# Odd periods of an attention loop: the second piece of the two-piece score tile goes to TensorE third instead of fourth, the first dense half product fourth

## The chip, the cores and the metric

One Trainium2 chip, one core of it. The metric is device microseconds of the whole program. Before the change three runs took 1686.16, 1686.31 and 1686.96 us; their median is 1686.31 us.

## The reference

Everything is float32, with one batch of S = 2048 tokens, width D = 512, 32 heads of 16 channels, and a gated hidden layer of F = 1792.

```python
def _A_ref(x, wqkv, wo):                                   # softmax attention, 32 heads of 16
    qkv = ((x @ wqkv).reshape(B, S, 3, H, Dh)).transpose(2, 0, 3, 1, 4)
    q, k, v = qkv[0], qkv[1], qkv[2]
    scores = einsum("bhqd,bhkd->bhqk", q, k) * Dh ** -0.5
    p = softmax(scores, axis=-1)
    o = einsum("bhqk,bhkd->bhqd", p, v)
    return o.transpose(0, 2, 1, 3).reshape(B, S, D) @ wo

def _B_ref(x, w_gate, w_up, w_down):                       # gated hidden layer
    return (sigmoid(x @ w_gate) * (x @ w_up)) @ w_down

g = sigmoid((x * gate_w).sum(-1, keepdims=True))           # one gate per token
out = g * _A_ref(x, wqkv, wo) + (1 - g) * _B_ref(x, w_gate, w_up, w_down)
```

## The kernel before, in words

**Stages.** A start (to about 85 us) makes the queries, keys and values that the first head pair needs. Then comes a long loop of 256 periods, `for k in range(NPER)`, and after it a last stage with the down projection and the output projection. The change is inside the first 248 periods (`NPER - TAIL`), which use the two strings of `STEADY`; the last eight use `LAST`, which is not touched.

**What a period does.** The heads are worked on in 16 pairs, each pair in 16 periods. A period handles, for the pair, 512 queries against 512 keys, and on TensorE it holds four kinds of work:

- *score tiles* (`t0`, `t1`; L641 in `st_part`): key rows times query columns, one 128x512 tile into a PSUM bank. ScalarE (ACT) takes each tile out with an exponential (L643, into `p`). Each period runs two calls of `st_part`, of four tiles each. The first tile of each period is written in two pieces of 192 and 320 columns (`CUT`), each with its own bank and its own exponential, so a period has nine score matmuls and nine exponentials.
- *maximum tiles* (`m0`, `m1`; L299 in `sm_step`): scores once more with the queries as rows, 128x512, some periods ahead of their use; VectorE (DVE) takes the row maxima (L301, into `stat`). Eight per period.
- *dense half products* (`d0`, `d1`; L153 and L173, into the one bank `dn`): projections of queries and keys, then the gate and up projections, then the start of the down projection, each contracting over 64 of the 128 rows. Twelve per period. ACT takes a finished `dn` out (L574).
- *value products* (L781 in `values`): 32 small matmuls after the written order of the period, with exponentials as their moving operand: those of the first score call of this period and of the second call of the period before. ACT copies the result out (L786), into `sum` for the first of four periods of a part and into `part` for the other three, which POOL then adds.

**Two halves of the array.** Tokens with a 0 use the lower 64 rows of TensorE's array, tokens with a 1 the upper 64, and the two halves work at the same time. In even periods the score tiles are on the lower half with six of the maximum tiles, and the dense products on the upper half; in odd periods it is the other way round.

**What sets the order.** All compute engines run what the program text emits, in that order (a manual schedule). `emit` reads a string of `STEADY` word by word, `STEADY[0]` for even k and `STEADY[1]` for odd k, and each word emits one matmul with what follows it (for `t` the matmul and its exponential on ACT, for `m` the matmul and its maximum on DVE, for `d` the matmul alone). The word `work` lets POOL take one of the jobs that wait in `later`. After the string come the run's change-over (`next(fill)`, with the copy out of `dn` on ACT), some POOL jobs, and `values(k)`.

**Banks.** Score tiles, maximum tiles and the value product take seven PSUM banks in turn (`place = turns(seven)`), each in the order in which it is emitted; a dense product takes no bank of these. A period takes 9 + 8 + 1 = 18 turns, so a matmul's bank is the one that was taken seven turns earlier, and it has to wait until ACT or DVE has read that one.

Of the kernel before, what the change touches and what calls it, by code (L numbers as in the profile page):

```python
# [51 lines left out]
def gated_mix(ctx, tc, x, xc, xmix, wqk, wv, wo, w_gu, w_down, gate_w, out):  # L52
# [768 lines left out]
    def emit(order, **parts):  # L821

        for word in order.split():
# [7 lines left out]
            else:  # L831
# [1 line left out]
                    place()  # L833

    STEADY = ("t0 m1 t0 d1 t0 d1 m0 d1 t0 m0 d1 d1 t0 d1 work t0 m0 d1 t0 d1 m0 d1 t0 d1 m0 d1 t0 d1 m1 m0",
              "t1 m0 d0 t1 t1 d0 m1 d0 t1 d0 m1 t1 d0 d0 work d0 t1 m1 t1 d0 d0 d0 m1 t1 d0 m1 t1 d0 m1 m0")
    LAST = ["t0 d1 t0 d1 t0 d1 t0 d1 d1 work t1 t1 t1 t1", "t0 d1 t0 d1 t0 d1 t0 d1 work t1 t1 t1 t1"] * 2 + [
        "t0 t0 t0 t0 work t1 d0 t1 d0 t1 d0 t1 d0 d0", "t0 t0 t0 t0 work t1 d0 t1 d0 t1 d0 t1 d0"] * 2

# [214 lines left out]
```

## Time and profile before

| what | before |
|---|---|
| median of 3 runs | 1686.31 us (1686.16 to 1686.96) |
| the profiled execution, its own time | 1686.26 us |
| its span in the trace | 1684.5 us |
| PE busy (matmuls) | 1678.5 us, 16842 instructions |
| DVE busy | 1429.2 us |
| ACT busy | 1346.9 us |
| POOL busy | 1054.2 us |

How to read it: the span is cut by engine into instructions. PE is TensorE's matmuls, PEld its weight loads, SP the queue that issues DMAs. A row of a timeline has the start in us from the span's start, the duration, the engine, the line of the kernel, the operation, the output and input tiles with their buffer numbers left out, and the count of instructions that were merged into the row; in square brackets stands the idle time of the engine ahead of it and what released it. Matmuls overlap in the pipeline and the end of each is modelled, so a PE that is busy all the time may still wait. A period is seen best on PE: each of the first 248 has exactly one 64x192 score matmul, its first instruction, so the distance between two of these is the length of a period.

### The profile page before, as it was taken

How to read it: one execution, taken by the hardware profiler on the slowest of the kernel's cores; microseconds unless marked ns; L12 is line 12 of the kernel's file. 1: busy time of each engine (PE TensorE's matmuls, PEld its weight loads, DVE VectorE, ACT ScalarE, POOL GpSimd, SP SyncE). 2: the span in 40 equal slices, each digit the busy share in tenths (PEclk: the TensorE clock that was granted, in tenths of full speed). 3: DMA queues.
4: the chain of work that ended last, by engine and by line, in shares of the span. 5: the costliest groups of instructions: out<-in, count | busy, mean ns of one | idle time of the engine just before them, and what ended most of it. 6: DMA issues, size and time to landing. Idle time of an engine off the chain costs nothing.

```text
span 1684.5 us, 44610 instructions
## 1 busy us (share of the span) xinstructions
PE 1678.5 (100%) x16842; PEld 1165.1 (69%) x16842; DVE 1429.2 (85%) x2456; ACT 1346.9 (80%) x2928; POOL 1054.2 (63%) x1238
## 2 busy tenths in 40 slices
PE   9999999999999999999999999999999999999999
PEld 7866666666666666666666666666666666678887
DVE  6889898898989989899898998989989899668553
ACT  4188888888888888888888999999999988974321
POOL 1146665368878788776675897777776767742110
PEclk9999999999999999999999999999999999999999
DMA  9624667464444444442347353424242325269850
GB/s 257 132 80 157 190 201 195 130 158 139 121 145 133 127 139 127 127 117 71 96 147 204 128 141 102 123 87 97 97 102 92 106 83 182 68 220 305 294 178 25
DMA packets 131559, 236.74 MB, mean 141 GB/s; under 512 B 19408, under 2 KB 39888, under 8 KB 128336
## 3 DMA queue, kind: packets, MB, share of 16 engines
q1 hardware_dynamic: 131056, 233.37, 46.5%
q8 instruction: 133, 2.18, 0.6%
q14 instruction: 82, 0.67, 0.2%
q10 hardware_dynamic: 288, 0.52, 0.1%
HBM read 155.71 MB, written 77.59 MB: 139 GB/s over the span
## 4 chain that ended last, share of the span: by engine, by line
PE 99%; DVE 0%; ACT 0%; issue 0%; POOL 0%; ACTq 0%; DVEq 0%
PE dn L173 27%; PE sm L781 17%; PE st L781 12%; PE dn L153 8%; PE sm L299 7%; PE sm L990 6%; PE sm L641 6%; PE st L299 5%; PE st L641 4%; PE st L140 4%; PE dn L990 2%; PE st L153 1%; PE st L990 1%; PE st L88 0%; DVE stat L301 0%; ACT p L643 0%
## 5 line engine op out<-in xcount | busy, mean ns | idle before, releaser
L301 DVE TENSOR_REDUCE stat<-sm 128x1 f32<-128x512 f32 x1199 | 763.8, 682 | 85.6 <-PE st L641 56.1
L643 ACT ACTIVATE p<-sm 128x512 f32<-128x512 f32 (+1 forms) x1314 | 669.6, 588 | 6.8 <-PE sm L641 5.3
L301 DVE TENSOR_REDUCE stat<-st 128x1 f32<-128x512 f32 x849 | 549.8, 682 | 57.8 <-PE sm L641 57.4
L643 ACT ACTIVATE p<-st 128x512 f32<-128x512 f32 (+2 forms) x982 | 515.6, 588 | 1.8 <-PE st L641 0.5
L299 PE MATMUL sm<-ks,qs 48*128 48x512 f32 x1199 | 486.1, 429 | 0.1
L173 PE MATMUL dn<-xm,mh 64*128 64x512 f32 x1568 | 486.1, 390 | 0.0
L641 PE MATMUL sm<-qs,ks 64*128 64x512 f32 (+1 forms) x1314 | 471.5, 382 | 0.0
L299 PE MATMUL st<-ks,qs 48*128 48x512 f32 x849 | 365.7, 431 | 0.0
L641 PE MATMUL st<-qs,ks 64*128 64x512 f32 (+2 forms) x982 | 363.0, 382 | 0.6 <-DVE v L622 0.6
L173 PE MATMUL dn<-xm,ml 64*128 64x512 f32 x784 | 305.4, 389 | 0.0
L173 PEld LDWEIGHTS dn<-xm,mh 64*128 64x128 f32 x1568 | 289.5, 185 | 14.5
L641 PEld LDWEIGHTS sm<-qs,ks 64*128 64x128 f32 x1314 | 233.1, 186 | 75.5 <-DVE stat L301 58.4
L781 PE MATMUL sm<-p,v 128*17 128x256 f32 x4672 | 280.6, 380 | 0.1
L299 PEld LDWEIGHTS sm<-ks,qs 48*128 48x128 f32 x1199 | 211.0, 184 | 45.5 <-ACT p L643 38.9
L641 PEld LDWEIGHTS st<-qs,ks 64*128 64x128 f32 x982 | 177.0, 186 | 57.5 <-DVE stat L301 44.9
L781 PEld LDWEIGHTS sm<-p,v 128*17 128x17 f32 x4672 | 122.9, 97 | 130.2 <-ACT p L643 44.6
L781 PE MATMUL st<-p,v 128*17 128x256 f32 x3520 | 211.4, 380 | 0.2 <-ACT p L643 0.2
L799 POOL TENSOR_TENSOR sum<-sum,part 128x256 f32<-128x256 f32 x192 | 141.5, 737 | 78.8 <-ACT part L786 62.7
L424 POOL TENSOR_TENSOR m<-m,m 128x512 f32<-128x512 f32 x140 | 178.0, 1289 | 5.4 <-ACT m L574 3.3
L299 PEld LDWEIGHTS st<-ks,qs 48*128 48x128 f32 x849 | 156.5, 184 | 32.3 <-ACT p L643 29.2
L781 PEld LDWEIGHTS st<-p,v 128*17 128x17 f32 x3520 | 92.7, 97 | 98.3 <-ACT p L643 33.5
L173 PEld LDWEIGHTS dn<-xm,ml 64*128 64x128 f32 x784 | 144.2, 184 | 10.0
(314 smaller groups left out, 2342.3 us busy)
## 6 DMA issues: line engine op xcount, KB each, us to landing
r<-in_w_gu_dram SPq DMA_DIRECT2D x112, 256.0 KB
gul<-gu_d SPq DMA_DIRECT2D x56, 512.0 KB
gu_d<-m SPq DMA_DIRECT2D x84, 256.0 KB
xm_d<-xm SPq DMA_DIRECT2D x32, 512.0 KB
xm<-xm_d SPq DMA_DIRECT2D x32, 512.0 KB
xm<-in_xmix_dram SPq DMA_DIRECT2D x24, 512.0 KB
qs<-q_d SPq DMA_DIRECT2D x90, 128.0 KB
ks<-k_d SPq DMA_DIRECT2D x90, 128.0 KB
```

The source lines that it names most:

```text
L140: pe.matmul(o, a, b, start=(i == 0), stop=(i == len(ops) - 1))
L153: mm = pe.matmul(self.o, a[rows], b[rows], start=(self.n == 0), stop=(self.n == 2 * len(self.ops) - 1))
L173: pe.matmul(self.o, a, b, start=(self.n == 0), stop=(self.n == len(self.ops) - 1))
L299: pe.matmul(t, qs[r:r + KM, qt * P:(qt + 1) * P], ks[r:r + KM, g * 512:(g + 1) * 512], start=True, stop=True)
L301: dve.tensor_reduce(stat[part][:, qt % 4, g:g + 1], t, axis=AX.X, op=ALU.max)
L424: pool.tensor_tensor(o, x, y, op)
L641: pe.matmul(o, ks[r:r + KR, (kt + a) * P:(kt + a + 1) * P], qs[r:r + KR, c * 512 + lo:c * 512 + hi], start=True, stop=True)
L643: act.activation(pt[:, a, lo:hi], o, AF.Exp, scale=DH ** -0.5)
L781: pe.matmul(o[r:r + VW, :], v[:, 4 * k % 16 + a, h * VW:(h + 1) * VW], pts[b][:, a, 256 * i:256 * i + 256], start=(a == 0), stop=(a == 3))
L799: pool.tensor_tensor(s, s, e, ALU.add)
L990: pe.matmul(down[t], a, b, start=(f == 0 and m == 0), stop=(f == NF - 2 and m == 5))
```

## The change

In the string for odd periods two neighbouring words change places: `t1 m0 d0 t1 t1 d0 ...` becomes `t1 m0 t1 d0 t1 d0 ...`. The third matmul of an odd period is then the 320-column second piece of the score tile, and the fourth the first dense half product. The string for even periods, which begins `t0 m1 t0 d1 t0 d1`, is as it was.

```diff
     STEADY = ("t0 m1 t0 d1 t0 d1 m0 d1 t0 m0 d1 d1 t0 d1 work t0 m0 d1 t0 d1 m0 d1 t0 d1 m0 d1 t0 d1 m1 m0",
-              "t1 m0 d0 t1 t1 d0 m1 d0 t1 d0 m1 t1 d0 d0 work d0 t1 m1 t1 d0 d0 d0 m1 t1 d0 m1 t1 d0 m1 m0")
+              "t1 m0 t1 d0 t1 d0 m1 d0 t1 d0 m1 t1 d0 d0 work d0 t1 m1 t1 d0 d0 d0 m1 t1 d0 m1 t1 d0 m1 m0")
```

The order of the instructions on TensorE differs in 124 places, one in each odd period; the orders on ACT, DVE, POOL and SP are the same as before. The score pieces and maximum tiles keep their order among themselves, so every one of them keeps its bank.

The first such place, at the opening of period 1 on TensorE (`dn` is the bank of the dense products, `q1h` a weight of the query projection, `st` and `sm` the seven banks in turn):

```order
 L641 MATMUL st1_66<-qs0_101,ks0_102 128x192
 L299 MATMUL sm3_72<-ks0_102,qs0_101 128x512
+L641 MATMUL st0_65<-qs0_101,ks0_102 128x320
 L153 MATMUL dn_68<-xt0_130,q1h_366 128x512
-L641 MATMUL st0_65<-qs0_101,ks0_102 128x320
 L641 MATMUL sm0_69<-qs0_101,ks0_102 128x512
```

The 320-column piece has moved ahead of one dense product.

In the middle of the program, at the opening of period 129 on TensorE (the dense products are now those of the up projection, L173), before:

```order
L641 MATMUL sm3_72<-qs0_101,ks0_102 128x192
L299 MATMUL st0_65<-ks0_102,qs0_101 128x512
L173 MATMUL dn_68<-xm0_2_4461,mh2_0_5_1_11185 128x512
L641 MATMUL sm0_69<-qs0_101,ks0_102 128x320
L641 MATMUL sm1_70<-qs0_101,ks0_102 128x512
L173 MATMUL dn_68<-xm0_2_4461,mh2_0_5_1_11185 128x512
L299 MATMUL st2_67<-ks0_102,qs0_101 128x512
```

and with the change:

```order
L641 MATMUL sm3_72<-qs0_101,ks0_102 128x192
L299 MATMUL st0_65<-ks0_102,qs0_101 128x512
L641 MATMUL sm0_69<-qs0_101,ks0_102 128x320
L173 MATMUL dn_68<-xm0_2_4461,mh2_0_5_1_11185 128x512
L641 MATMUL sm1_70<-qs0_101,ks0_102 128x512
L173 MATMUL dn_68<-xm0_2_4461,mh2_0_5_1_11185 128x512
L299 MATMUL st2_67<-ks0_102,qs0_101 128x512
```

The same two instructions have changed places, with the same banks.

The opening of period 130, an even one, on TensorE, the same before and after:

```order
L641 MATMUL st2_67<-qs0_101,ks0_102 128x192
L299 MATMUL sm2_71<-ks0_102,qs0_101 128x512
L641 MATMUL st1_66<-qs0_101,ks0_102 128x320
L173 MATMUL dn_68<-xm0_2_4461,mh2_0_5_1_11185 128x512
L641 MATMUL sm3_72<-qs0_101,ks0_102 128x512
L173 MATMUL dn_68<-xm0_2_4461,mh2_0_5_1_11185 128x512
L299 MATMUL st0_65<-ks0_102,qs0_101 128x512
```

Nothing moved here; it stands for comparison, since an odd period now opens with the same kinds of instructions in the same order.

## The prediction

> **What bounds the kernel now.** I read the page first, then the list of waits, and then the timeline of two neighbouring periods engine by engine.
>
> ```profile
> span 1684.5 us, 44610 instructions
> PE 1678.5 (100%) x16842; PEld 1165.1 (69%) x16842; DVE 1429.2 (85%) x2456; ACT 1346.9 (80%) x2928; POOL 1054.2 (63%) x1238
> PEld sm L781 <- ACT p L643: 44.6, 146, 0.5
> PEld st L781 <- ACT p L643: 33.5, 109, 0.7
> ```
>
> The page makes PE busy all the time, but these are modelled ends. The waits say more: the value products (L781) waited for an exponential 146 + 109 = 255 times, which is once in each period but one. So every period ends with PE behind ACT, and the question is what ACT does in a period. First PE's timeline: an odd period (129, from 802.01) and the even one after it (from 807.60), to the start of the next.
>
> ```profile
> 802.01 0.35 PE L641 MATMUL sm<-qs,ks 64*128 64x192 f32 x1
> 802.01 0.50 PE L299 MATMUL st<-ks,qs 48*128 48x512 f32 x1
> 802.20 0.33 PE L641 MATMUL sm<-qs,ks 64*128 64x320 f32 x1
> 802.35 0.39 PE L173 MATMUL dn<-xm,mh 64*128 64x512 f32 x1
> ...
> 804.71 0.39 PE L299 MATMUL st<-ks,qs 48*128 48x512 f32 x1
> ...
> 804.88 0.39 PE L173 MATMUL dn<-xm,ml 64*128 64x512 f32 x1
> 804.94 0.39 PE L641 MATMUL sm<-qs,ks 64*128 64x512 f32 x1
> 805.26 0.50 PE L299 MATMUL st<-ks,qs 48*128 48x512 f32 x1
> 805.26 0.50 PE L299 MATMUL sm<-ks,qs 48*128 48x512 f32 x1
> 805.75 1.92 PE L781 MATMUL sm<-p,v 128*17 128x256 f32 x32
> 807.60 0.35 PE L641 MATMUL st<-qs,ks 64*128 64x192 f32 x1
> ...
> 807.94 0.40 PE L173 MATMUL dn<-xm,mh 64*128 64x512 f32 x1
> ...
> 811.24 1.92 PE L781 MATMUL sm<-p,v 128*17 128x256 f32 x32
> 813.09 0.35 PE L641 MATMUL st<-qs,ks 64*128 64x192 f32 x1
> ```
>
> The odd period lasts 807.60 - 802.01 = 5.59 us, the even one 813.09 - 807.60 = 5.49. From the value products to the next period both take 1.85 us (805.75 to 807.60, 811.24 to 813.09); the difference of 0.10 lies before them: 3.74 us in the odd period, 3.64 in the even one. Both hold nine score matmuls, eight maximum tiles and twelve dense products. It is not these two periods alone; the openings of periods 2 and 246 give the mean of the 122 pairs between them:
>
> ```profile
> 97.83 0.35 PE L641 MATMUL sm<-qs,ks 64*128 64x192 f32 x1
> 1450.62 0.35 PE L641 MATMUL st<-qs,ks 64*128 64x192 f32 x1
> ```
>
> (1450.62 - 97.83) / 122 = 11.09 us a pair. With 5.49 for the even period an odd one is 5.60 in the mean.
>
> Now ACT, the same two periods, in narrow windows so that rows aren't merged: the copy of the last value product, the exponentials of 192 and 320 columns, and the sixth and seventh exponential.
>
> ```profile
> 802.14 0.38 ACT L786 ACTIVATE sum<-st 128x256 f32<-128x256 f32 x1 [0.57 <-PE st L781]
> 802.46 0.33 ACT L643 ACTIVATE p<-sm 128x192 f32<-128x192 f32 x1
> 802.81 0.44 ACT L643 ACTIVATE p<-sm 128x320 f32<-128x320 f32 x1
> 804.58 0.63 ACT L643 ACTIVATE p<-st 128x512 f32<-128x512 f32 x1
> 805.05 0.65 ACT L643 ACTIVATE p<-sm 128x512 f32<-128x512 f32 x1
> ...
> 807.80 0.38 ACT L786 ACTIVATE part<-sm 128x256 f32<-128x256 f32 x1 [0.63 <-PE sm L781]
> 808.08 0.33 ACT L643 ACTIVATE p<-st 128x192 f32<-128x192 f32 x1
> 808.29 0.45 ACT L643 ACTIVATE p<-st 128x320 f32<-128x320 f32 x1
> 810.04 0.66 ACT L643 ACTIVATE p<-sm 128x512 f32<-128x512 f32 x1
> ```
>
> The value product's bank was taken seven turns earlier by the seventh score piece, so it starts when the seventh exponential is through: 805.05 + 0.65 = 805.70, and PE goes at 805.75. In between ACT runs without a break, a 512-column exponential every 0.47 us (804.58 to 805.05). A period is thus one chain: value product, its copy, seven exponentials, next value product. Whatever holds an early exponential is paid in full at the end.
>
> The two chains differ at one place. In the odd period ACT starts the 320-column exponential 0.35 us after the 192-column one (802.46, 802.81), and after that one's end (802.79). In the even period it starts 0.21 after it (808.08, 808.29), overlapping its last 0.12, as all later steps overlap (each 0.63 to 0.66 long, 0.47 apart). So in the odd period ACT is held by the 320-column matmul, and in the even one it isn't.
>
> **The change, part by part.** It removes and adds nothing; per odd period the 320-column piece goes ahead of one dense product. Three effects.
>
> *The 320-column exponential is released earlier.* In the odd period this matmul is emitted behind the dense product; that one ends at 802.35 + 0.39 = 802.74, and the exponential starts 0.07 later. In the even period the dense product is behind it and the exponential starts 808.29 - 807.94 = 0.35 after the dense product's start, before that has ended. The recorded start of the 320-column matmul itself (802.20) is ahead of the dense product (802.35), against the emitted order; I believe ACT's start, since ACT is what the chain waits for, and take it that the count ACT waits on passes the 320-column piece after the dense one. The Trainium skill, TensorE: Matmul & The Clock Gate, section "The mechanism", says that matmuls start and end strictly in program order; the ends seem to agree (released 0.07 us after the dense product's end), the recorded starts don't. By that rule the sum would be the same.
>
> The even period is then the price list for the changed odd one: 5.60 - 5.49 = 0.11 us saved.
>
> *Some odd periods can do better.* In period 129 the copy goes to `sum` and ACT takes it 0.13 us after the period's start (802.01, 802.14); a copy to `part` in period 130 comes at 0.20 (807.60, 807.80). In the odd period this head start is lost, since ACT then waits for the 320 columns anyway. A few even periods have the early copy; this one opens at 430.84:
>
> ```profile
> 430.84 0.35 PE L641 MATMUL sm<-qs,ks 64*128 64x192 f32 x1
> 430.98 0.38 ACT L786 ACTIVATE part<-st 128x256 f32<-128x256 f32 x1 [0.57 <-PE st L781]
> 431.29 0.33 ACT L643 ACTIVATE p<-sm 128x192 f32<-128x192 f32 x1
> 431.52 0.43 ACT L643 ACTIVATE p<-sm 128x320 f32<-128x320 f32 x1
> 436.30 0.35 PE L641 MATMUL sm<-qs,ks 64*128 64x192 f32 x1
> L786 ACT ACTIVATE sum<-sm 128x256 f32<-128x256 f32 x35 | 13.4, 384 | 20.6 <-PE sm L781 20.6
> L786 ACT ACTIVATE sum<-st 128x256 f32<-128x256 f32 x27 | 10.4, 384 | 15.3 <-PE st L781 15.3
> ```
>
> It copies at 0.14, starts the 320 columns at 0.68 (0.69 in the even period above, 0.80 in the odd one) and lasts 436.30 - 430.84 = 5.46 us. There are 35 + 27 = 62 copies to `sum`; `values` makes one after every fourth period, from 0 on, so it falls into the opening of an odd one. Hence 62 of the 124 odd periods come to 5.46, a saving of 0.14, and the other 62 to 5.49.
>
> *The dense product goes one place back.* It stays behind the same maximum tile on its half of the array and in the even period starts at 807.94 - 807.60 = 0.34, as in the odd one (802.35 - 802.01). The 320 columns' own bank has long been read. I cost it at nothing, covered by the maximum tile that runs ahead of it on the same half for 0.50 us; without that cover it would be the 0.2 us of the slower rival. Nothing is issued on SP or POOL by the words that change places.
>
> One period saves nothing: in the one that opens at 247.49 (its copy is at 247.62) the first exponential itself is late.
>
> ```profile
> 247.62 0.38 ACT L786 ACTIVATE sum<-sm 128x256 f32<-128x256 f32 x1 [1.06 <-PE sm L781]
> 248.22 0.33 ACT L643 ACTIVATE p<-st 128x192 f32<-128x192 f32 x1 [0.22 <-PE sm L641]
> ```
>
> The sum: 62 x 0.14 = 8.7, plus 62 x 0.11 = 6.8, less 0.1 for that period: 15.4 us. The profiled execution took 1686.26 us around a span of 1684.5, the median is 1686.31; they agree to 0.05, so the saving counts against either: 1686.3 - 15.4 = **1670.9 us**.
>
> Bounds for a period's saving. Above: 0.14, the shift of the exponential itself (0.35 less 0.21) and the shortest even period; 124 x 0.14 = 17.4 us, 1668.9. Below: ACT's visible gap in the odd period is only 802.81 - 802.79 = 0.02, if the overlap of the two exponentials can't be had there; 124 x 0.02 = 2.5 us, 1683.8. I take the even period's value, since it is measured on the same instructions with only the array halves exchanged.
>
> What is late next? DVE idles at the opening of both periods, so it has room for 0.14:
>
> ```profile
> 802.54 0.69 DVE L301 TENSOR_REDUCE stat<-st 128x1 f32<-128x512 f32 x1 [0.61 <-PE sm L641]
> 808.14 0.69 DVE L301 TENSOR_REDUCE stat<-sm 128x1 f32<-128x512 f32 x1 [0.45 <-PE st L641]
> ```
>
> POOL is busy for 63% of the span.
>
> **The rivals.**
>
> *PE's own pace takes over.* In the odd period the last two maximum tiles start at 805.26, 0.32 after the last score tile; at PE's step of 0.23 (804.71 to 804.94) they could at best go at 805.17. If that 0.09 is all, the gain is 124 x 0.09 = 11.2 us: 1675.1. Against it: the 5.46 us period has the same number of matmuls on each half.
>
> *No effect.* If the recorded starts are the truth, the array already runs the 320 columns (802.20) ahead of the dense product (802.35), and the late exponential has another cause that belongs to the odd order or the upper half. Then the time stays at 1686.3. Against it: the exponential's start just behind the dense product's end.
>
> *Slower: the piece blocks its own half's weights.* Emitted directly behind the 192 columns on the same half, it may have to wait until these are through (0.35) and its weights are in (0.19 to the next start, 802.01 to 802.20), and the dense product behind it would start at 0.54 instead of 0.34. Its half then still has that product, eleven more and a maximum tile to run; the last of these, due 0.23 after the last dense product (804.88), goes 0.20 later, at 805.31 instead of 805.26: 0.05 x 124 = 6.2 us, 1692.5. It decides as soon as the delay is over 0.15. Against it: the even period opens in this order and its dense product starts at 0.34. The Trainium skill, same page and section, has it that a weight load overlaps a running matmul only if the two are on different row groups, which would make this rival real; the even period disagrees, with the 0.34.
>
> **How the numbers follow.** Forecast as summed (1668.9 to 1673): 0.74. PE's pace or another part of the gain (1673 to 1682): 0.12. No effect: 0.09. Slower: 0.05. A measurement of this kernel can tell about 0.2%, 3.4 us, from no change. The first two cases are faster by more than that: 0.86; same 0.09; slower 0.05. The range takes the forecast's own bounds and the first rival's 1675.1 with some room: 1668.5 to 1677.
>
> **What would show it.** In the changed profile odd periods should open as even ones do: the 320-column exponential 0.21 to 0.23 us after the 192-column one, the value products 3.61 to 3.64 us after the period's start, and periods of 5.46 (after `sum`) and 5.49. The recorded starts on PE should hardly move. The pair falls from 11.09 to 10.96 in the mean. I am wrong if the exponential still starts 0.35 behind the first; or if it starts early and the value products still wait until 3.74, for another reason; or if the dense product starts at over 0.4.

## The result, and the profile after

The changed kernel took **1671.09 us** (median of 4 runs, 1670.84 to 1671.81) against 1686.24 us for the kernel before (4 runs, 1685.29 to 1686.96): a ratio of 0.9911, 95% interval 0.9894 to 0.9928. The profiled execution has a span of 1669.2 us, 15.3 less than the 1684.5 before.

The page and the waits of the changed kernel, in the lines that answer to those shown of before:

```profile
span 1669.2 us, 44610 instructions
PE 1663.4 (100%) x16842; PEld 1174.6 (70%) x16842; DVE 1427.2 (85%) x2456; ACT 1334.1 (80%) x2928; POOL 1052.3 (63%) x1238
PEld sm L781 <- ACT p L643: 44.6, 146, 0.5
PEld st L781 <- ACT p L643: 33.5, 109, 0.6
```

The counts of instructions and the 255 waits of the value products for an exponential are the same; what shrank is the time from one such wait to the next. PE's timeline, periods 129 and 130 again, and the openings of periods 131, 2 and 246:

```profile
794.03 0.35 PE L641 MATMUL sm<-qs,ks 64*128 64x192 f32 x1
794.04 0.50 PE L299 MATMUL st<-ks,qs 48*128 48x512 f32 x1
794.23 0.33 PE L641 MATMUL sm<-qs,ks 64*128 64x320 f32 x1
794.38 0.39 PE L173 MATMUL dn<-xm,mh 64*128 64x512 f32 x1
...
797.16 0.50 PE L299 MATMUL sm<-ks,qs 48*128 48x512 f32 x1
797.20 0.45 PE L299 MATMUL st<-ks,qs 48*128 48x512 f32 x1
797.64 0.41 PE L781 MATMUL sm<-p,v 128*17 128x256 f32 x4
...
799.49 0.35 PE L641 MATMUL st<-qs,ks 64*128 64x192 f32 x1
...
804.98 0.35 PE L641 MATMUL st<-qs,ks 64*128 64x192 f32 x1
...
97.48 0.35 PE L641 MATMUL sm<-qs,ks 64*128 64x192 f32 x1
1435.44 0.35 PE L641 MATMUL st<-qs,ks 64*128 64x192 f32 x1
```

The odd period 129 now lasts 799.49 - 794.03 = 5.46 us (5.59 before), the even one 804.98 - 799.49 = 5.49, as before. The pair is (1435.44 - 97.48) / 122 = 10.97 us in the mean (11.09 before). The value products start 797.64 - 794.03 = 3.61 us into the odd period (3.74 before). The recorded starts at the opening have not moved: 320 columns 0.20 after the 192, the dense product at 0.35.

ACT in the same odd period: copy, both pieces, seventh exponential; then the copy and the pieces of period 131, an odd one that opens at 804.98 with a copy to `part`:

```profile
794.17 0.39 ACT L786 ACTIVATE sum<-st 128x256 f32<-128x256 f32 x1 [0.57 <-PE st L781]
794.48 0.33 ACT L643 ACTIVATE p<-sm 128x192 f32<-128x192 f32 x1
794.71 0.43 ACT L643 ACTIVATE p<-sm 128x320 f32<-128x320 f32 x1
...
796.93 0.66 ACT L643 ACTIVATE p<-sm 128x512 f32<-128x512 f32 x1
...
805.18 0.38 ACT L786 ACTIVATE part<-sm 128x256 f32<-128x256 f32 x1 [0.63 <-PE sm L781]
805.46 0.33 ACT L643 ACTIVATE p<-st 128x192 f32<-128x192 f32 x1
805.67 0.45 ACT L643 ACTIVATE p<-sm 128x320 f32<-128x320 f32 x1
```

The 320-column exponential starts 0.68 us into period 129 (0.80 before), 0.23 after the 192-column one (0.35 before), and now overlaps its end (794.48 + 0.33 = 794.81). In period 131 it starts at 0.69, 0.21 after. The seventh ends at 796.93 + 0.66 = 797.59, and the value products go 0.05 later, as before.

DVE, the first maximum of periods 129 and 130:

```profile
794.57 0.69 DVE L301 TENSOR_REDUCE stat<-st 128x1 f32<-128x512 f32 x1 [0.62 <-PE sm L641]
800.03 0.69 DVE L301 TENSOR_REDUCE stat<-sm 128x1 f32<-128x512 f32 x1 [0.31 <-PE st L641]
```

Its idle time ahead of the even period's first maximum fell from 0.45 to 0.31 us and is not used up.

### The profile page after: what moved, and what is told of

Read it like the earlier page. It is cut to its first block, busy times and chain, and to the rows that moved or that the text cites. A ratio compares the mean times of both kernels' runs of the same rounds, so it can differ in the third digit from the quotient of the medians.

```text
span 1669.2 us, 44610 instructions
## 1 busy us (share of the span) xinstructions
PE 1663.4 (100%) x16842; PEld 1174.6 (70%) x16842; DVE 1427.2 (85%) x2456; ACT 1334.1 (80%) x2928; POOL 1052.3 (63%) x1238
## 4 chain that ended last, share of the span: by engine, by line
PE 99%; DVE 0%; ACT 0%; issue 0%; POOL 0%; ACTq 0%; DVEq 0%
PE dn L173 27%; PE sm L781 17%; PE st L781 13%; PE dn L153 7%; PE sm L299 6%; PE sm L641 6%; PE sm L990 6%; PE st L299 4%; PE st L641 4%; PE st L140 4%; PE dn L990 2%; PE st L153 2%; PE st L990 1%; PE st L88 0%; ACT p L643 0%; DVE stat L301 0%
## 5 line engine op out<-in xcount | busy, mean ns | idle before, releaser
L173 PE MATMUL dn<-xm,mh 64*128 64x512 f32 x1568 | 485.7, 389 | 0.0
L173 PE MATMUL dn<-xm,ml 64*128 64x512 f32 x784 | 304.7, 389 | 0.0
L173 PEld LDWEIGHTS dn<-xm,mh 64*128 64x128 f32 x1568 | 290.0, 185 | 15.9
L173 PEld LDWEIGHTS dn<-xm,ml 64*128 64x128 f32 x784 | 144.4, 184 | 10.3
```

Of the source, the lines that this page charges most:

```text
L173: pe.matmul(self.o, a, b, start=(self.n == 0), stop=(self.n == len(self.ops) - 1))
```

## The experiments

Six kernels ran. The first four were timed beside the kernel before at 1686.10 us (13 runs), the last two beside it at 1686.01 us (15 runs).

### The other half of the array: the old order in even periods

```diff
-    STEADY = ("t0 m1 t0 d1 t0 d1 m0 ...
+    STEADY = ("t0 m1 d1 t0 t0 d1 m0 ...
```

> The changed kernel, with the even periods opened as the odd ones were before (t0 m1 d1 t0 t0 d1): one dense product ahead of the 320-column piece, on the other halves of the array. Theory (one dense product ahead holds the 320-column exponential, whichever half): even periods go from 5.49 to 5.60 us, 124 x 0.11 = 13.6 us, 1684.7 us in all; the 320-column exponential in even periods starts at 0.80 instead of 0.69. Rival (it was something of the odd periods or the upper half): no change, 1671.1 us.

Measured: 1684.49 us (10 runs, 1683.79 to 1684.82), ratio to the kernel before 0.9990 [0.9981, 0.9999]; 13.4 us over the changed kernel where 13.6 were expected. PE at the opening of the even period 130 and of the next, and ACT's 320-column exponential in it:

```profile
806.72 0.35 PE L641 MATMUL st<-qs,ks 64*128 64x192 f32 x1
...
812.31 0.35 PE L641 MATMUL st<-qs,ks 64*128 64x192 f32 x1
...
807.52 0.44 ACT L643 ACTIVATE p<-st 128x320 f32<-128x320 f32 x1
```

The even period lasts 5.59 us and the exponential starts at 0.80. What cost time was the order, not something of odd periods or of the upper half; the even period was a fair price list. That this kernel is still 1.6 us under the kernel before also fits: the early copies to `sum` all open odd periods, which can now use them, and 62 periods of 5.46 us in place of 5.49 make about 1.4 us.

### A larger dose: two dense products ahead

```diff
-              "t1 m0 t1 d0 t1 d0 m1 d0 ...
+              "t1 m0 d0 d0 t1 t1 m1 d0 ...
```

> The changed kernel, with two dense products ahead of the 320-column piece in odd periods (t1 m0 d0 d0 t1 t1). Theory: the exponential is released by the end of the last dense product ahead, one step of 0.23 us later than with one: it starts at 0.58 + 0.39 + 0.07 = 1.04 us, odd periods take 5.60 + 0.23 = 5.83 us, 1686.2 + 124 x 0.23 = 1714.7 us. If the piece itself only had to start after the dense products: its end at 0.58 + 0.33 = 0.91, the exponential at 0.98, 124 x 0.06 less: 1707 us. Rival (order plays no part, the halves run apart): near 1686 us or below.

Measured: 1715.18 us (2 runs, 1714.84 to 1715.53), ratio 1.0173 [1.0153, 1.0193]. The opening of period 129 on PE, and ACT:

```profile
817.37 0.35 PE L641 MATMUL sm<-qs,ks 64*128 64x192 f32 x1
...
817.57 0.33 PE L641 MATMUL sm<-qs,ks 64*128 64x320 f32 x1
817.71 0.40 PE L173 MATMUL dn<-xm,mh 64*128 64x512 f32 x1
...
817.95 0.39 PE L173 MATMUL dn<-xm,mh 64*128 64x512 f32 x1
...
818.42 0.44 ACT L643 ACTIVATE p<-sm 128x320 f32<-128x320 f32 x1 [0.26 <-PE st L299]
```

The trace still puts the 320-column matmul at 817.57 to 817.90, but its exponential starts at 818.42, 1.05 us into the period, 0.08 after the second dense product's end (817.95 + 0.39 = 818.34). By these times ACT would have idled 0.26 us for nothing (the releaser named in the bracket, a maximum tile, is inferred from recorded ends). 1.04 was expected for a release by the end of what stands ahead, 0.98 for a release after its start.

### A short matmul ahead

An extra word `e0` between `m0` and the 320-column piece runs this method of `Side`, the class of the gate and up projections:

```diff
+        def probe(self):
+            if self.n == 0:
+                a, b = self.ops[0]
+                pe.matmul(self.o[:, :128], a, b[:, :128], start=True, stop=True)
...
-              "t1 m0 t1 d0 t1 d0 m1 ...
+              "t1 m0 e0 t1 d0 t1 d0 m1 ...
```

> The changed kernel, with an extra matmul of 128 columns of the first dense product's operands ahead of the 320-column piece, in the 98 odd periods of the gate and up projections; the product itself then overwrites it, so nothing is left out. Theory (the exponential is released by the end of what stands ahead): the short matmul starts at 0.34 and ends near 0.57, before ACT is free; the exponential starts at 0.67 to 0.69 as now, 1671 to 1673 us. Rival (the piece can't start before what stands ahead of it has started, at 0.34, so its size doesn't matter): the exponential starts near 0.74 to 0.80, 98 x 0.06 to 0.12 = 6 to 12 us, 1677 to 1683 us.

Measured: 1671.01 us (4 runs, 1670.48 to 1671.51), ratio 0.9910 [0.9893, 0.9926]. Period 129 (L179 is the added matmul; lines after it are shifted by some):

```profile
794.30 0.35 PE L646 MATMUL sm<-qs,ks 64*128 64x192 f32 x1
...
794.64 0.22 PE L179 MATMUL dn<-xm,mh 64*128 64x128 f32 x1
...
794.71 0.44 PE L173 MATMUL dn<-xm,mh 64*128 64x512 f32 x1
...
794.98 0.43 ACT L648 ACTIVATE p<-sm 128x320 f32<-128x320 f32 x1
```

The short matmul takes the place that the dense product had, starts at the same 0.34 and ends at 794.86, 0.56 us into the period. The exponential starts at 0.68. So it isn't the position behind a matmul of the other half that costs, nor that one's start, but its end: with 512 columns that came at 0.73, too late for ACT; with 128 columns it comes in time.

### One place further: the piece second

```diff
-              "t1 m0 t1 d0 t1 d0 m1 ...
+              "t1 t1 m0 d0 t1 d0 m1 ...
```

> The changed kernel, with the 320-column piece ahead of the first maximum tile too in odd periods (t1 t1 m0 d0). Theory: ACT is busy with the copy and the 192-column exponential until 0.67 us, so nothing more is to be had on its chain. If the halves of the array start apart from each other: the maximum tile starts at 0.00 as now, 1671.1 us. If starts are strictly in the emitted order: the maximum tile starts at 0.19, its half is 0.19 late to the end and the value products at least 0.10 us later: 1671.1 + 12.4 = 1683.5 us.

Measured: 1671.21 us (4 runs, 1670.78 to 1671.54), ratio 0.9912 [0.9897, 0.9927], no different from the change. PE and DVE in period 129, and ACT's 320-column exponential:

```profile
793.82 0.35 PE L641 MATMUL sm<-qs,ks 64*128 64x192 f32 x1
793.83 0.50 PE L299 MATMUL sm<-ks,qs 48*128 48x512 f32 x1
794.01 0.33 PE L641 MATMUL st<-qs,ks 64*128 64x320 f32 x1
...
794.42 0.69 DVE L301 TENSOR_REDUCE stat<-sm 128x1 f32<-128x512 f32 x1 [0.67 <-PE st L641]
...
794.50 0.43 ACT L643 ACTIVATE p<-st 128x320 f32<-128x320 f32 x1
```

The exponential stays at 0.68: ACT has nothing more to gain there. The maximum tile is recorded at the period's start, ahead of the piece that is emitted before it; it isn't 0.19 late, and the 12.4 us of that case are not there. But its consumer is released later: DVE starts at 0.60 instead of 0.54, 0.08 after the end of the 320-column piece (794.01 + 0.33 = 794.34). That is the same rule with the parts exchanged, on DVE, where the slack pays; the counts of TensorE's semaphore, given with the release below, bear it out.

### What is next on ACT's chain: the copy's second wait

The prediction found that a copy to `part` starts 0.06 us later than one to `sum`. Most copies to `part` wait for PE and also for POOL, which long since has read the buffer. The wait for POOL is put on an exponential at the end of a period, where ACT has a queue of work:

```diff
+    adds = []
...
-                act.activation(pt[:, a, lo:hi], o, AF.Exp, scale=DH ** -0.5)
+                e = act.activation(pt[:, a, lo:hi], o, AF.Exp, scale=DH ** -0.5)
+                if a == 3 and not first and len(adds) > 1:
+                    tc.add_manual_dep(e.ins, adds[-2].ins.name, SYNC, reason="part is free")
...
-            pool.tensor_tensor(s, s, e, ALU.add)
+            adds.append(pool.tensor_tensor(s, s, e, ALU.add))
```

> The changed kernel; the wait for POOL that 173 copies of the value product carry as a second wait (so that part is free again) is put on the last exponential of the period before the copy. Theory (ACT's chain still sets the period, and the second wait costs the copy 0.06 us, of which 5.49 - 5.46 = 0.024 us reaches the period): 173 x 0.024 = 4.2 us, 1666.9 us; late copies start 0.14 us after the period's start instead of 0.20, and nearly all periods take 5.46 us. Rival (PE's own pace now sets the period, and 5.46 is only had where the banks fall well): 1671.1 us.

Measured: **1667.10 us** (4 runs, 1666.68 to 1667.38), ratio to the kernel before 0.9887 [0.9874, 0.9901]; 4.0 us under the changed kernel where 4.2 were expected. Period 130, its copy, and the opening of the next:

```profile
797.42 0.35 PE L642 MATMUL st<-qs,ks 64*128 64x192 f32 x1
797.55 0.38 ACT L789 ACTIVATE part<-sm 128x256 f32<-128x256 f32 x1 [0.57 <-PE sm L784]
802.88 0.35 PE L642 MATMUL st<-qs,ks 64*128 64x192 f32 x1
```

The copy starts at 0.13 (0.20 before), idle 0.57 instead of 0.63 behind the value product, and the period lasts 5.46 us. Over periods 1 to 246, the 171 copies with the second wait start at 0.20 in the changed kernel (one of them at 0.47), while the 75 without it, 13 of them to `part`, start at 0.14; here all 246 start at 0.14. So the wait made the copy late, not the tile that it writes. ACT's chain still set the length of the periods that had the late copy. Only part of the 0.06 us arrives: the 192-column exponential starts 0.48 us into a period with the late copy and 0.45 into one with the early copy, and the period differs by about 0.02; what takes up the rest isn't shown. This version is faster than both kernels.

The same edit on the kernel before:

> The kernel before, with the same moved wait as the run before. Theory (in odd periods the 320-column exponential waits for PE at 0.80 us, so an earlier copy is lost there): only the 117 late even periods gain, 117 x 0.024 = 2.8 us, 1683.4 us; odd periods stay at 5.60 us. Rival (the head start counts in all periods): 173 x 0.024 = 4.2 us, 1682.0 us, with late odd periods at 5.57.

Measured: 1682.87 us (11 runs, 1682.11 to 1683.45), ratio 0.9982 [0.9973, 0.9991]. The gain, 3.1 us under this series' 1686.01, lies between the two that were expected, 2.8 and 4.2, and the time alone doesn't settle it. The trace does: periods 129 to 131, with the copy and the 320-column exponential of the odd period 131:

```profile
804.85 0.35 PE L642 MATMUL st<-qs,ks 64*128 64x192 f32 x1
...
810.31 0.35 PE L642 MATMUL st<-qs,ks 64*128 64x192 f32 x1
810.45 0.38 ACT L789 ACTIVATE part<-sm 128x256 f32<-128x256 f32 x1 [0.57 <-PE sm L784]
811.12 0.44 ACT L644 ACTIVATE p<-sm 128x320 f32<-128x320 f32 x1
815.91 0.35 PE L642 MATMUL sm<-qs,ks 64*128 64x192 f32 x1
```

The even period falls to 810.31 - 804.85 = 5.46 us; the odd one stays at 815.91 - 810.31 = 5.60, although its copy now starts at 0.14, because the exponential still waits for PE until 0.81. The value product's bank is read earlier in these periods too, so that alone brings nothing. In the old order a head start on ACT was lost in odd periods, as the prediction had it.

## Why the prediction was right

*The bound.* ACT's chain from one value product to the next sets the period: confirmed by the moved wait, which only lets ACT's copy start earlier and brings 4.0 us, and by the larger dose, where a delay of about 0.24 us at the second exponential (median of the odd periods 1.04 instead of 0.81) makes the time 1715.18 - 1686.10 = 29.1 us longer, 124 x 0.235.

*The release.* The prediction took it that the 320-column exponential is released only when the dense product ahead of it has ended, against the recorded starts. The consumers agree in every run: none ahead or a short one, ACT's own 0.68; one, 0.80; two, 1.05. The trace also holds what ACT waits for, the times at which TensorE's semaphore counts (`updates` in the packed trace, which no view prints). An event does not name its matmul, so the table goes by the order of emission. It has medians over the 123 odd periods from 1 to 245 (for the short matmul, over the 98 that have it), in us from the period's start:

| emitted ahead of the piece | counted last before it, at | the piece, recorded end | the piece, counted | its exponential starts |
|---|---|---|---|---|
| one dense product (before) | dense product 0.75 | 0.52 | 0.79 | 0.81 |
| none (the change) | maximum tile 0.52 | 0.52 | 0.55 | 0.68 |
| two dense products | second dense product 0.99 | 0.52 | 1.02 | 1.04 |
| a matmul of 128 columns | short matmul 0.58 | 0.52 | 0.61 | 0.68 |

In the kernel before there is no event at all between 0.52 and 0.73 us in any of these periods, so the piece wasn't counted at its recorded end, and ACT starts 0.02 us after the count that comes next behind the dense product's. In the changed kernel the count comes well before ACT is free. With the piece second, the piece is counted at 0.54, the maximum tile behind it at 0.57, and DVE starts at 0.59.

The Trainium skill (TensorE: Matmul & The Clock Gate, section "The mechanism") says that matmuls start and end strictly in program order. The counts agree with the ends: 0.75 for the dense product, 0.79 for the piece emitted behind it. The recorded starts don't agree: 0.34 for the dense product, 0.19 for the piece. Whether the piece's result lay in its bank before it was counted stays open, since consumers go by the count.

*The two prices.* 5.46 us for the odd periods after a copy to `sum` and 5.49 for the others were both met (the medians over all 62 and over the other 61 up to period 246), and the even periods kept their length. The odd periods from 1 to 245 alone are 14.9 us shorter in sum, so the saving of 15.2 us (1686.24 to 1671.09) was made where the forecast of 15.4 put it. The one miss is too small for the time to show: a second odd period, at 1278.63 before and 1265.31 after, also has a late first exponential and saved nothing.

*The rivals.* PE's own pace did not take over: the last maximum tiles went at 797.16 and 797.20, 3.13 and 3.17 us into the period instead of 3.25; the rival's earliest start, 805.17 or 3.16 us into the period, was no floor for the first of them. "No effect" fell with the result, and its cause, something of the upper half, with the first experiment, since the old order costs the same in even periods. The slower rival, a piece that blocks its own half's weights, would have moved the dense product to 0.54; it starts at 0.35. DVE had the slack that was quoted, and kept 0.31 us of it.

## What to carry to other kernels

Two halves of TensorE's array ran side by side here, and a tile was given free in the order of emission. In such a kernel, put a short matmul that a busy chain waits for ahead of a long one that nobody waits for, even if the two don't share rows. Read the release from the consumer's start, not from the recorded start and end of the matmul. If a period occurs in two forms with the same work and one is shorter, line up their chains instruction by instruction; the first place where they part is where to look, and here the difference of the two lengths was the price.

## What the runs showed of the hardware

The recorded starts of matmuls on the two halves don't follow the emitted order, and they don't move when it changes: the 320-column piece is recorded about 0.20 us after the 192-column one with no, one or two dense products emitted ahead of it, while its consumer starts at 0.68, 0.80 and 1.05 us. The semaphore's counts do follow the emitted order: a piece with a recorded end of 0.52 was counted at 0.55, 0.79 and 1.02, in the last two cases 0.03 us after the dense product ahead of it. And a copy on ACT with a second wait, long fulfilled, started 0.06 us later than one without when ACT stood idle ahead of it (0.63 against 0.57 us of idle time); the trace has a separate semaphore instruction of ACT's sequencer ahead of every such copy. On a busy ACT, where the wait was moved, it cost nothing that the period shows.
